# Ordering attention-value matmuls by key block over four PSUM slots, with a re-planned instruction list

## The chip, the cores and the metric

One core of one Trainium2 chip. The metric is device microseconds of one execution; the runs before took 289.94 us in the median (289.79 to 290.12). Every execution also leaves a span, from its first to its last profiled instruction, which is shorter than the time (by 1.8 us in the profiled run before). TensorE is the engine that multiplies matrices, ScalarE (ACT) takes the exponentials, VectorE (DVE) the masks and normalisations.

## The reference, cut to what matters

```python
scores = scale * np.matmul(q, k.transpose(0, 1, 3, 2))     # q, k, v: 4 x 8 x 768 x 64
scores = np.where(mask, scores, -1000000000.0)             # window, edge and random blocks of 32
attn = exp(scores - max) / sum                             # [cut: softmax]
x = np.matmul(attn, v)                                     # -> 3072 tokens x 512
gate = 1.0 / (1.0 + np.exp(-(x @ w_gate)))                 # 512 x 1536
return (gate * (x @ w_val)) @ w_out
```

Of the kernel before, what the change touches and what calls it, by code (L numbers as in the profile page):

```python
# [18 lines left out]
NJ = S // 128  # L19
# [8 lines left out]
VW = 96  # L28
SPIN = 22.0
NMASK = 1  # L30
SEED, MIX = 43, 0.4
WANT, READY = 4, 1
Q0P, M1P, M2P = -39.2, 14, 17
XR, HR, HOLD, HN = 3, 2, 0.4, 1
# [236 lines left out]
def kernel(  # L271
# [33 lines left out]
    P = Plan()  # L305
# [11 lines left out]
    def sb(tag, shape, dt):  # L317
        n = len(P.rings[tag])
        return Buf(tag, lambda i: work.tile(shape, dt, tag=tag, bufs=n, name=tag))
# [4 lines left out]
    def psb(shape, dt=f32, homes=SINGLE, span=1):  # L324
        def make(i):
            t = psum[:, i : i + span].rearrange("p b c -> p (b c)")
            if dt != f32:
                t = t.bitcast(dt)
            n = int(np.prod(shape))
            t = t[:, 0:n]  # L330
            if len(shape) == 2:
                t = t.rearrange("p (a b) -> p a b", a=shape[0])
            return t

        b = Buf("ps", make)
        b.homes, b.span = homes, span
        return b
# [23 lines left out]
    for i, (eng, q, r) in enumerate((("SP", nc.sync, 0), ("ACT", nc.scalar, 64))):  # L361
# [3 lines left out]
            writes=[e24], prio=-93, dma=0.2, lands=LAND[f"e{i}"],  # L365
        ).deps[1:] = []
    vring = [one([128, 2, NJ, VW], f16, f"v16_{i}") for i in range(8)]
    for i in range(8):
# [3 lines left out]
            writes=[vring[i]], prio=-80 + i,  # L372
# [15 lines left out]
    stage, half16, tr, v16 = {}, {}, {}, {}  # L388
    landed = {}

    def load(nm, b, p, prio, after=(), sync=None, behind=()):
        t = sb(f"{nm}s", [128, 2, NJ, 64], f32)
        stage[nm, b, p] = t

        def go():
            ins = nc.sync.dma_start(t(), src[nm][b][:, 2 * p : 2 * p + 2])
            if sync is not None:
                tc.add_manual_dep(
                    ins.ins, landed[sync].ins.name,
                    mybir.DependencyInfo(mybir.DependencyClass.Sync, mybir.DependencyReason.DATA),  # L400
                    reason="later loads",
                )

        return P.op("SP", 0.5, go, writes=[t], prio=prio, after=after, behind=behind, dma=1.07)
# [111 lines left out]
    n = 0  # L516
    for a, z in zip(edges, edges[1:]):
        for nm, t, s in (("g", wg, wgv), ("v", wv, wvv)):
# [4 lines left out]
            o = P.op("POOL", 0.75, go, prio=-37.5 + n * 0.75, behind=[last_in], dma=32 * (0.022 + (z - a) * 0.000124))  # L523
# [100 lines left out]
    valued, scored = {}, []  # L624

    def attend(n, p, seq):
        b, c = divmod(n, NCH)
        masked = n < NMASK
        pts = []
        for tt in range(NCH):  # L630
            st, pt = psb([2, 512], homes=PAIR, span=2), sb("pt", [128, 2, 2, CH], f16)

            def scores(tt=tt, st=st):
                qT, kT = tr["q", b, p](), tr["k", b, p]()
                for jj in range(2):
                    for own in (0, 1) if masked else (1,):
                        for hd in range(2):
                            r = slice(hd * 64, hd * 64 + 64)
                            l, m = (kT, qT) if own else (e24(), bias())
                            nc.tensor.matmul(  # L640
                                st()[:, hd, jj * CH : (jj + 1) * CH],
                                l[r, 2 * tt + jj, :],
                                m[r, 2 * c : 2 * c + 2, :],
                                start=not (own and masked), stop=bool(own),
                            )

            need = [tr["q", b, p], tr["k", b, p]]
            o = P.op(
                "PE", 0.43 if masked else 0.215, scores, reads=[*need, e24, bias] if masked else need,
                writes=[st], prio=seq, mode="row", behind=scored[-1:],  # L650
            )
            if (n, p, tt) == (0, 0, 0):
                o.deps.remove(late)
            scored.append(o)
            o.paired, o.twin = (n, p) not in EARLY and 4 * n + p < CHAIN, psb([2, 512], homes=PAIR, span=2)
            P.op(
                "ACT", 0.915,
                lambda st=st, pt=pt: nc.scalar.activation(  # L658
                    pt().rearrange("p h j q -> p h (j q)"), st(), AF.Exp, scale=SCALE
                ),  # L660
                reads=[st], writes=[pt], prio=seq,
            )

            def masks(tt=tt, pt=pt):
                t = pt().rearrange("p h j q -> p h (j q)")
                nc.vector.tensor_tensor(  # L666
                    t, t, mask()[:, c, tt].unsqueeze(1).to_broadcast([128, 2, 512]), op=ALU.mult
                )

            if not masked:  # L670
                P.op("DVE", 0.61, masks, reads=[pt], writes=[pt], after=[mask_ops[c, tt]], prio=seq)
            pts.append(pt)

        o, rz, x16 = psb([4, 128]), sb("rz", [128, 4, 1], f32), sb("x16", [128, 2, 128], f16)

        def values():
            v_ = v16[b, p]()
            for jq in range(2):
                for hd in range(2):
                    for j in range(NJ):  # L680
                        nc.tensor.matmul(  # L681
                            o()[:, 2 * jq + hd, 0:65],
                            pts[j // 2]()[:, hd, j % 2, jq * 128 : jq * 128 + 128],
                            v_[:, hd, j, 0:65],
                            start=(j == 0), stop=(j == NJ - 1),
                        )

        valued[n, p] = P.op("PE", 0.79, values, reads=[*pts, v16[b, p]], writes=[o], prio=seq + (3.05 if n == 0 and p < 3 else 0.1), mode="full")
        hold = HOLD if n < HN else 0.0
        P.op(  # L690
            "DVE", 0.2, lambda: nc.vector.reciprocal(rz(), o()[:, :, 64:65]), reads=[o], writes=[rz], prio=seq - 5  # L691
        ).hold = hold
        P.op(
            "DVE", 0.36,
            lambda: nc.vector.tensor_tensor(  # L695
                x16().rearrange("p j (h d) -> p (j h) d", d=64),
                o()[:, :, 0:64],
                rz().to_broadcast([128, 4, 64]),
                op=ALU.mult,
            ),  # L700
            reads=[o, rz], writes=[x16], prio=seq - 5,
        ).hold = hold
        g, i = group_of[n]
        dst = xT[g, p]
        if n >= TURN_PE:
            P.op(
                "SP", 1.2,
                lambda: nc.sync.dma_start_transpose(
                    dst()[:, i * CH : (i + 1) * CH].rearrange("p (j q) -> p j q", j=2),
                    x16().rearrange("p j m -> p (j m)"),  # L710
                ),
                reads=[x16], writes=[dst], prio=seq - 5, dma=0.45,
            )
            return
        tT = psb([2, 128], f16)

        def turn():
            dst()
            for jq in range(2):
                nc.tensor.transpose(tT()[:, jq, :], x16()[:, jq, :], ident16())  # L720

        P.op("PE", 0.12, turn, reads=[x16, ident16], writes=[tT, dst], prio=seq - 5, mode="full").hold = hold
        P.op(
            "DVE", 0.28,
            lambda: nc.vector.tensor_copy(
                dst()[:, i * CH : (i + 1) * CH], tT().rearrange("p j q -> p (j q)")
            ),
            reads=[tT], writes=[dst], prio=seq - 5,
        ).hold = hold
# [90 lines left out]
    seq, turned, late_loads = 0, [], []  # L820
    order = [(n, p) for n in range(B * NCH) for p in range(NP)]
    order = EARLY + [i for i in order if i not in EARLY]
    for n, p in order:
        b, c = divmod(n, NCH)
# [10 lines left out]
        if p == NP - 1 and b + 1 < B and c == 0:  # L835
            for p in range(NP):
                for nm in "kqv":
                    o = load(
                        nm, b + 1, p, seq + p, behind=turned[:-2][-2:],
                        **(dict(after=[w_out[4]], sync="o") if b == 0 else {}),  # L840
                    )
# [71 lines left out]
```

## The kernel before: what the change and the argument touch

The kernel records operations with planned durations. A planner then walks in time through these durations and fixes the order of instructions on each engine. Priorities get a random shift, drawn from a seed, so that the seed and the durations together choose the list. Where TensorE has nothing to do before 22 us, the planner inserts a filler matmul on zeros (44 in the trace of before, the last at 22.4 us).

One attention block is one chunk of 256 queries of one pair of heads. It has three score tiles (768 keys), whose exponentials lie in `pts`, and then one values block: 24 matmuls, each 128 keys by 128 queries times 65 columns. Column 65 of `v` is ones, so that it sums the denominators. The four results (two query tiles times two heads) lie in four slots of one PSUM bank.

```python
SEED, MIX = 43, 0.4
...
def run(self):
    mix = np.random.default_rng(SEED).normal(0.0, MIX, len(self.ops))
    for i, o in enumerate(self.ops):
        o.key = (o.prio + (mix[i] if -45 < o.prio < 60 else 0.0), i)
...
def spin_op(dur, fresh):                       # the filler, "L380"
    ...
    return P.op("PE", dur, lambda: nc.tensor.matmul(t()[0:64], zero()[:, 0:64], zero(), start=True, stop=True), ...)
...
o, rz, x16 = psb([4, 128]), ...                # four slots of 128 columns in one bank

def values():                                  # "L681"
    v_ = v16[b, p]()
    for jq in range(2):
        for hd in range(2):
            for j in range(NJ):                # NJ = 6 key blocks
                nc.tensor.matmul(
                    o()[:, 2 * jq + hd, 0:65],
                    pts[j // 2]()[:, hd, j % 2, jq * 128 : jq * 128 + 128],
                    v_[:, hd, j, 0:65],
                    start=(j == 0), stop=(j == NJ - 1),
                )

valued[n, p] = P.op("PE", 0.79, values, reads=[*pts, v16[b, p]], writes=[o], ...)
```

`start` is given to the matmul that begins a sum; I call that a clear, and here a block has four. L640 are the score matmuls, L746 the gate and value products of the feed-forward part, L791 its output product, L720 and L457 transposes.

The softmax here doesn't subtract the row's maximum and nothing guards it: scores larger than these inputs give would overflow.

## Time and profile before

| | |
|---|---|
| time, median of 3 | 289.94 us |
| span of the profiled run | 288.5 us |
| TensorE busy, matmuls | 98% of the span, 3030 |
| values matmuls (L681) | 1152, in 48 blocks of 24 |
| a values block, start to next start | 0.73 us |
| a steady period (one attention block and its share of the feed-forward part) | 5.48 us |
| fillers (L380) | 44 |

The prediction below shows the lines behind most of these. For a full engine the step from one start to the next start is the cost; a row's own duration overlaps what follows (the values row at 153.84 us is 0.89 us long, and the next row starts after 0.73 us).

These are the first score matmuls in the timeline of the kernel before (start in us, duration in us, engine, line, operation, output and inputs, count):

```profile
6.30 0.28 PE L640 MATMUL psum<-bias,e 64*128 64x256 f16 x2
6.42 0.27 PE L640 MATMUL psum<-qT,kT 64*128 64x256 f16 x2
6.53 0.27 PE L640 MATMUL psum<-bias,e 64*128 64x256 f16 x2
6.64 0.27 PE L640 MATMUL psum<-qT,kT 64*128 64x256 f16 x2
...
8.00 0.41 PE L457 MATMUL psum<-ident,q_late 128*64 128x128 f16 x8
```

Pairs of score matmuls, whose two members start 3 to 4 ns apart, follow each other every 0.11 us here, and the twelve pairs are over at 8.0 us.

### The profile page before, as it was taken

How to read it: one execution, taken by the hardware profiler on the slowest of the kernel's cores; microseconds unless marked ns; L12 is line 12 of the kernel's file. 1: busy time of each engine (PE TensorE's matmuls, PEld its weight loads, DVE VectorE, ACT ScalarE, POOL GpSimd, SP SyncE). 2: the span in 40 equal slices, each digit the busy share in tenths (PEclk: the TensorE clock that was granted, in tenths of full speed). 3: DMA queues.
4: the chain of work that ended last, by engine and by line, in shares of the span. 5: the costliest groups of instructions: out<-in, count | busy, mean ns of one | idle time of the engine just before them, and what ended most of it. 6: DMA issues, size and time to landing. Idle time of an engine off the chain costs nothing.

```text
span 288.5 us, 7279 instructions
## 1 busy us (share of the span) xinstructions
PE 282.4 (98%) x3030; PEld 172.7 (60%) x3030; DVE 186.7 (65%) x401; ACT 204.3 (71%) x281; POOL 14.9 (5%) x24
## 2 busy tenths in 40 slices
PE   7998999999999999999999999999999999999995
PEld 6686786787578555555555555554555555447753
DVE  3788997898897876876586575476476474223310
ACT  3969879987897898886888886876776773333321
POOL 8740000000000000000000000000000000000000
PEclk9999999999999999999999999999999999999999
DMA  7999999992799982061867661101011012001013
GB/s 111 171 207 211 208 242 257 239 286 57 220 211 172 258 203 50 18 184 36 227 179 161 218 69 56 33 25 55 21 38 55 11 47 57 36 36 36 19 56 111
DMA packets 50785, 35.25 MB, mean 122 GB/s; under 512 B 31376, under 2 KB 47808, under 8 KB 50752
## 3 DMA queue, kind: packets, MB, share of 16 engines
q1 hardware_dynamic: 43304, 27.71, 37.5%
q0 software_dynamic: 7232, 7.01, 15.2%
q8 instruction: 23, 0.38, 0.6%
q10 hardware_dynamic: 216, 0.07, 0.1%
q14 instruction: 10, 0.08, 0.1%
HBM read 28.42 MB, written 6.29 MB: 120 GB/s over the span
## 4 chain that ended last, share of the span: by engine, by line
PE 93%; DMA 2%; ACT 2%; POOL 2%; issue 0%; ACTq 0%; POOLq 0%
PE psum L746 44%; PE psum L791 23%; PE psum L640 13%; PE psum L681 12%; DMA q<-in_q_dram 2%; ACT pt L658 1%; PE psum L457 1%; PE psum L720 1%; POOL k L439 0%; PE psum L602 0%; POOL k_a L486 0%; POOL q_late L439 0%; POOL q L439 0%; POOL k_b L490 0%; PE psum L380 0%
## 5 line engine op out<-in xcount | busy, mean ns | idle before, releaser
L658 ACT ACTIVATE pt<-psum 128x1024 f16<-128x1024 f32 x144 | 138.8, 1029 | 25.1 <-PE psum L640 25.1
L666 DVE TENSOR_TENSOR pt<-pt,mask 128x1024 f16<-128x1024 f16 x132 | 88.9, 686 | 45.7 <-ACT pt L658 45.6
L746 PE MATMUL psum<-x,wv 128*128 128x256 f16 (+1 forms) x384 | 78.2, 326 | 0.0
L746 PE MATMUL psum<-x,wg 128*128 128x256 f16 (+1 forms) x384 | 78.2, 326 | 0.0
L767 ACT ACTIVATE tg<-psum 128x256 f32<-128x256 f32 (+1 forms) x96 | 47.6, 499 | 41.7 <-PE psum L746 30.6
L791 PE MATMUL psum<-wo,h 128*128 128x512 f16 (+2 forms) x300 | 73.0, 371 | 0.0
L774 DVE SCALAR_TENSOR_TENSOR h<-tg,psum 128x256 f16<-128x256 f32 (+1 forms) x96 | 52.2, 550 | 28.8 <-PE psum L746 16.1
L746 PEld LDWEIGHTS <-wg 128*128 128x128 f16 x384 | 35.9, 98 | 24.3 <-issue 1.7
L746 PEld LDWEIGHTS <-wv 128*128 128x128 f16 x384 | 35.3, 98 | 23.0 <-issue 2.5
L681 PEld LDWEIGHTS <-pt 128*128 128x128 f16 x1152 | 41.0, 97 | 8.8 <-issue 1.1
L640 PE MATMUL psum<-qT,kT 64*128 64x256 f16 x576 | 45.0, 271 | 0.5 <-ACT pt L658 0.4
L791 PEld LDWEIGHTS <-h 128*128 128x128 f16 x300 | 26.3, 98 | 30.2 <-issue 5.7
L681 PE MATMUL psum<-v,pt 128*128 128x65 f16 x1152 | 42.7, 193 | 0.3 <-ACT pt L658 0.3
L640 PEld LDWEIGHTS <-kT 64*128 64x128 f16 x576 | 24.5, 94 | 18.6 <-issue 15.4
L695 DVE TENSOR_TENSOR x<-psum,rz 128x256 f16<-128x256 f32 x48 | 20.4, 424 | 1.7
L809 ACT ACTIVATE y<-psum 128x512 f32<-128x512 f32 (+2 forms) x22 | 12.7, 579 | 10.9 <-PE psum L791 10.8
L691 DVE RECIPROCAL rz<-psum 128x4 f32<-128x4 f32 x48 | 8.6, 179 | 4.9 <-PE psum L681 4.8
L380 PE MATMUL psum<-zero 128*64 128x128 f16 x44 | 6.1, 287 | 1.0 <-DVE zero L350 1.0
L427 ACT CAST q<-qs 128x768 f16<-128x768 f32 x8 | 6.8, 845 | 0.0
L610 DVE TENSOR_SCALAR mask<-psum 128x512 f16<-128x512 f32 x9 | 6.0, 684 | 0.5 <-PE psum L640 0.5
L640 PE MATMUL psum<-bias,e 64*128 64x256 f16 x48 | 6.0, 273 | 0.0
L380 PEld LDWEIGHTS <-zero 128*64 128x64 f16 x44 | 4.6, 155 | 2.1 <-issue 1.1
(54 smaller groups left out, 72.3 us busy)
## 6 DMA issues: line engine op xcount, KB each, us to landing
out_dram<-y SPq DMA_DIRECT2D x23, 256.0 KB, 2.0
qs<-in_q_dram SPq DMA_DIRECT2D x12, 384.0 KB, 3.8
vs<-in_v_dram SPq DMA_DIRECT2D x12, 384.0 KB, 4.9
ks<-in_k_dram SPq DMA_DIRECT2D x12, 384.0 KB, 4.5
wg<-in_moe_w_gate_dram POOLq DMA_DIRECT2D x2, 768.0 KB, 13.9
wv<-in_moe_w_val_dram POOLq DMA_DIRECT2D x2, 768.0 KB, 16.0
wo<-in_moe_w_out_dram POOLq DMA_DIRECT2D x3, 512.0 KB, 21.9
vh<-in_v_dram POOLq DMA_DIRECT2D x4, 192.0 KB, 8.1
```

What stands on the lines that cost most here:

```text
L380: "PE", dur, lambda: nc.tensor.matmul(t()[0:64], zero()[:, 0:64], zero(), start=True, stop=True),
L640: nc.tensor.matmul(st()[:, hd, jj * CH : (jj + 1) * CH], l[r, 2 * tt + jj, :], m[r, 2 * c : 2 * c + 2, :], start=not (own and masked), sto ...
L658: lambda st=st, pt=pt: nc.scalar.activation(pt().rearrange("p h j q -> p h (j q)"), st(), AF.Exp, scale=SCALE),
L666: nc.vector.tensor_tensor(t, t, mask()[:, c, tt].unsqueeze(1).to_broadcast([128, 2, 512]), op=ALU.mult)
L681: nc.tensor.matmul(o()[:, 2 * jq + hd, 0:65], pts[j // 2]()[:, hd, j % 2, jq * 128 : jq * 128 + 128], v_[:, hd, j, 0:65], start=(j == 0), ...
L691: "DVE", 0.2, lambda: nc.vector.reciprocal(rz(), o()[:, :, 64:65]), reads=[o], writes=[rz], prio=seq - 5
L695: lambda: nc.vector.tensor_tensor(x16().rearrange("p j (h d) -> p (j h) d", d=64), o()[:, :, 0:64], rz().to_broadcast([128, 4, 64]), op=AL ...
L746: nc.tensor.matmul(t()[:, z : z + w], wt()[:, i, f * 128 : (f + 1) * 128], xT[g, i]()[:, 0:w], start=(i == 0), stop=(i == NP - 1),)
L767: lambda tg=tg, a=pair[0]: nc.scalar.activation(tg()[:, 0:w], a[0]()[:, a[1] : a[1] + w], AF.Tanh, scale=0.5),
L774: lambda tg=tg, a=pair[1], h_=h_: nc.vector.scalar_tensor_tensor(h_()[:, 0:w], tg()[:, 0:w], 1.0, a[0]()[:, a[1] : a[1] + w], op0=ALU.add, ...
L791: nc.tensor.matmul(py()[:, m], hts[g, f]()[:, tt * 128 : (tt + 1) * 128], wo()[:, f, m], start=(f == 0), stop=(f == NF - 1),)
L809: lambda py=py, y=y, m=m: nc.scalar.activation(y()[:, m], py()[:, m], AF.Copy, scale=0.5),
```

## The change

Its intent: six matmuls in a row that add to the same 65 columns were thought to be slower than matmuls that go round over the four slots. All four sums are now open at once in one bank, and the first matmul alone has `start`. The planned duration of a block goes down with it, and with a new seed the planner makes another list.

```diff
-SEED, MIX = 43, 0.4
+SEED, MIX = 3, 0.4
...
-            for jq in range(2):
-                for hd in range(2):
-                    for j in range(NJ):
+            for j in range(NJ):
+                for jq in range(2):
+                    for hd in range(2):
                         nc.tensor.matmul(
                             o()[:, 2 * jq + hd, 0:65],
                             pts[j // 2]()[:, hd, j % 2, jq * 128 : jq * 128 + 128],
                             v_[:, hd, j, 0:65],
-                            start=(j == 0), stop=(j == NJ - 1),
+                            start=(j + jq + hd == 0), stop=(j == NJ - 1), skip_group_check=True,
                         )
...
-        valued[n, p] = P.op("PE", 0.79, values, ...
+        valued[n, p] = P.op("PE", 0.715, values, ...
```

More of the change, by code (lines that the diff above doesn't have):

```diff
@@ L684, in values @@
                             v_[:, hd, j, 0:65],
-                            start=(j == 0), stop=(j == NJ - 1),
+                            start=(j + jq + hd == 0), stop=(j == NJ - 1), skip_group_check=True,
                         )
-        valued[n, p] = P.op("PE", 0.79, values, reads=[*pts, v16[b, p]], writes=[o], prio=seq + (3.05 if n == 0 and p < 3 else 0.1), mode="full")
+        valued[n, p] = P.op("PE", 0.715, values, reads=[*pts, v16[b, p]], writes=[o], prio=seq + (3.05 if n == 0 and p < 3 else 0.1), mode="full")
         hold = HOLD if n < HN else 0.0
```

## The prediction

> **What bounds the kernel now.** I read the page's busy shares first, then the slices, the chain that ended last, the waits of TensorE, and last the timeline of one period of the steady part. The first two lines and the slices of the page:
>
> ```profile
> span 288.5 us, 7279 instructions
> ## 1 busy us (share of the span) xinstructions
> PE 282.4 (98%) x3030; PEld 172.7 (60%) x3030; DVE 186.7 (65%) x401; ACT 204.3 (71%) x281; POOL 14.9 (5%) x24
> ...
> PE   7998999999999999999999999999999999999995
> ...
> PEclk9999999999999999999999999999999999999999
> ```
>
> TensorE (PE) is busy 98% of the span at a full granted clock, and only the first slice (loads still under way) and the last (copying out the end) fall short. The chain says the same:
>
> ```profile
> PE 93%; DMA 2%; ACT 2%; POOL 2%; issue 0%; ACTq 0%; POOLq 0%
> PE psum L746 44%; PE psum L791 23%; PE psum L640 13%; PE psum L681 12%; DMA q<-in_q_dram 2%; ACT pt L658 1%; PE psum L457 1%; PE psum L720 1%; POOL k L439 0%; PE psum L602 0%; POOL k_a L486 0%; POOL q_late L439 0%; POOL q L439 0%; POOL k_b L490 0%; PE psum L380 0%
> ```
>
> 93% of the chain is matmuls; the changed ones, the values matmuls of L681, are 12%, that is 0.12 x 288.5 = 35 us for 48 blocks of 24, or 0.72 us a block. All waits of TensorE together are five:
>
> ```profile
> PE psum L380 <- DVE zero L350: 1.0, 1, 1.0
> PE psum L578 <- DMA e<-bb_e: 0.6, 1, 0.6
> PE psum L640 <- ACT pt L658: 0.4, 1, 0.4
> PE psum L457 <- DMA k<-in_k_dram: 0.4, 1, 0.4
> PE psum L681 <- ACT pt L658: 0.3, 1, 0.3
> ```
>
> That is 2.7 us of idle, 2.0 of it in the first 10 us where loads rule. The two waits on ACT are at 24.8 and 27.4 us; in the table of busy time by stages TensorE has no idle time at all between 30 and 240 us. So a better list order can win back at most about 0.7 us of idle, and the rest of any gain must come from matmuls that take less time. One steady period:
>
> ```profile
> 153.40 0.60 PE L791 MATMUL psum<-wo,h 128*128 128x512 f16 x2
> 153.84 0.89 PE L681 MATMUL psum<-v,pt 128*128 128x65 f16 x24
> 154.57 1.02 PE L746 MATMUL psum<-x,wv 128*128 128x512 f16 x4
> 155.44 1.03 PE L746 MATMUL psum<-x,wg 128*128 128x512 f16 x4
> ...
> 159.32 0.89 PE L681 MATMUL psum<-v,pt 128*128 128x65 f16 x24
> ```
>
> The block's line (L681, 153.84) is to be read by its start: its 0.89 us includes its drain, which overlaps the next block; what the block costs the stream is the step to the next start, 154.57 - 153.84 = 0.73 us. The whole period is 159.32 - 153.84 = 5.48 us.
>
> [...] starts of L746 with 256 columns lie 109 ns apart [...], with 512 columns 216 ns [...]. [...] the trace's values blocks take 729 to 730 ns in the steady part, so 730/24 = 30.4 ns[...]. [...] each weight load of L681 starts about 2 ns after the matmul before it starts, and no matmul waits for one by record. [...]
>
> **Part 1: the order inside a values block.** Nothing is removed: 24 weight loads of 128x128 and 24 matmuls of 65 columns before and after, 1152 in all, with the same operands. Before, six matmuls in a row add to the same 65 columns; after, the same columns come round every fourth matmul [...]. Three first clears a block go, but in the trace's start-to-start steps those matmuls (7th, 13th, 19th) take no longer than others: a clear costs nothing visible. What is visible is a pattern: steps of 29 ns, and one of 35 after every four or so, while the records' durations creep from 191 to 196 ns between the long steps and fall back after each. I read this as issue at 29.2 ns a matmul into something downstream that takes 30.4 ns each, which pushes back now and then. Two candidates: the add to an address written one matmul ago (then the new order removes it), or the pace of weight loads and small outputs as such (then nothing changes).
> If it is the add, the block falls[...]; if issue alone is left, to 24 x 29.2 = 700 ns, 29 ns less. The planned figure in the diff (0.79 to 0.715) is not a measured step: before measures 0.73, not 0.79, so the 0.075 of the diff can't be what comes out[...].
> On the path: five blocks of L681 lie before 28 us, where ACT's exponentials set the pace (the chain gives 4.3 us to them from 23.45 us), so 43 of 48 count. [...] at most 43 x 0.029 = 1.25.
>
> **Part 2: the list order.** The built programs have equal counts of every matmul but the filler one: 44 before, 47 after. The fillers (L380) run where the planner finds nothing else, before 23 us; 3 more, at some 0.1 us, sit in time that is waited anyway, and one more pair of array-mode changes comes with them. Changes between full-array and row-paired matmuls cost about 95 ns each in the trace (a 512-column matmul takes 312 ns to the next start in place of 216). There are 55 + 53 = 108 of these in either program, so the new order saves none. From the fully chained part on (after about 125 us) the block order is the same in both. Between 20 and 125 us blocks are permuted. This can shift the 0.3 and 0.4 us waits on ACT, or make new ones: ACT is busy 22 of 25 us at 100 to 125 us, and DVE 18 of 20 at 60 to 80 us, so there is not much room. I put the sum at 0 with a spread of some 0.6 us, leaning to a small win since the plan now carries shorter times for TensorE's work.
> The tail, from the last matmul to the end, is unchanged: 288.5 - 285.3 = 3.2 us.
>
> Sum: [...] some 0.25 us for the list: 0.8 us off 289.94, so **289.1 us**.
>
> **Rivals.** First, order doesn't matter to the array: 30.4 ns is what a weight load and a small matmul take together. For it: the long steps come about every fifth matmul and do not line up with the slot borders at every sixth, where the same-address add is absent; weight-load records creep (96 to 100 ns) along with the matmuls. Against it: none shows as a wait. Time then 289.9, give or take the list. Second, the diff's own numbers are right and a block loses 0.075 us: 48 x 0.075 = 3.6 us, so 286.3 us. Against it: 0.73 - 0.075 = 0.655 us is 27.3 ns a matmul[...]. Third, the permuted middle part opens waits on ACT or DVE, of up to a few tenths each: 290 to 291 us. For it: ACT's and DVE's busy shares above; against it: the old plan, made with the same planner, left TensorE no idle there, and values that are really shorter only make the engine less hurried than planned. Fourth, key-block order lets the first eight matmuls start with the first score tile alone; but the wait before L681 is 0.3 us in the whole run, so this is worth nothing.
>
> **Range and chances.** Low end: all long steps gone (1.25) and the waits on ACT won back (0.7) is 288.0; 287.9 with a little over. High end: no gain, and 0.5 us of new waits: 290.4. Faster by over 2% would need 284.1 us, 5.8 us less, more than even the second rival; slower by over 2% needs 5.8 us of new waits in a part that has none. One chance in a hundred each.
>
> **What will show it.** The step from a values block to the next block (0.73 us in the steady part) should read 0.71, and the steady period 5.46 in place of 5.48; if both are unchanged, the first rival holds; at 0.66 and 5.41 the second. The long steps of 35 ns should be fewer or gone. TensorE's waits on ACT should stay at or below 0.7 us in sum; new rows after 30 us mean the third rival. Bank clears, mode changes, the tail and the first 12 us should be as before. The prediction is wrong if same-address adds cost nothing and the list brings waits, or if something else in the middle part gains more than the 0.7 us of idle that I see there.

The sum came to 0.8 us off 289.94: 0.56 for the loop order and some 0.25 for the list. The 0.56 was my estimate, two chances in three of a shorter block in 43 of the 48; the pace for a matmul of 65 columns that it rested on was not shown. The 0.71 and 5.46 us under "What will show it" rest on it too. The trace of before allows an estimate of its own: matmuls of 128 columns (L791) follow each other every 56 ns, of 256 (L746) every 109, of 512 every 216, so about 0.42 ns a column, and 63 columns fewer than 128 leave 56 - 26.5 = 29.5 ns, or 708 for a block; measured are 30.4 and 729 or 730. Against the second rival, which needs 27.3 ns a matmul, stands that no step inside a steady block of that trace is under 29 ns. That something downstream pushes back was a reading of the step times, which no run showed.

## The result, and the profile after

The changed kernel took 291.89 us in the median of four runs (291.54 to 292.31), against 290.02 us (289.79 to 290.12) for four runs of the kernel before. The ratio was 1.0066, with a 95% interval of 1.0049 to 1.0084. That is within 2%, slower instead of faster, and outside the predicted range.

The first check is the block itself. One steady period of the changed kernel, from its timeline:

```profile
149.50 0.90 PE L681 MATMUL psum<-v,pt 128*128 128x65 f16 x24
150.23 1.02 PE L746 MATMUL psum<-x,wg 128*128 128x512 f16 x4
...
154.99 0.90 PE L681 MATMUL psum<-v,pt 128*128 128x65 f16 x24
```

The period is now 154.99 - 149.50 = 5.49 us; before it was 5.48. From the trace's start times in ns, a steady block takes 735, where before it took 729 or 730. The block has not become shorter by 20 ns but longer by 6. The pauses of 35 ns are still there, and there is one more of them (steps between the 24 starts, and to the next block, of one block each):

```
before 30 35 29 29 29 29 35 29 30 29 29 35 29 29 29 30 35 29 29 29 29 35 29 | 30
after  29 35 29 29 29 35 29 30 29 35 29 29 29 29 35 30 29 29 29 35 29 29 30 | 35
```

The second check is TensorE's waits in the changed kernel (who waited for whom; us in total, times, longest):

```profile
PE psum L380 <- DVE zero L350: 1.0, 1, 1.0
PE psum L720 <- DVE x L695: 0.7, 1, 0.7
PE psum L578 <- DMA e<-bb_e: 0.6, 1, 0.6
PE psum L457 <- DMA k_b<-in_k_dram: 0.3, 1, 0.3
PE psum L681 <- ACT pt L658: 0.3, 1, 0.3
```

Their sum is 2.8 us by the trace's ns (the rows are rounded); it was 2.7. One wait for ACT (0.4 us before L640) has become one for DVE before a transpose (0.7 us before L720, at 27.7 us). After 30 us there is again no wait: the permuted middle part opened none.

The third check is where the span grew by 1.0 us. I cut both profiled runs at matmuls that both have: the first values matmul, the first feed-forward matmul (L746), the first matmul of the 48th values block, and the last matmul of all.

| us | before | after |
|---|---|---|
| span's start to first values matmul | 14.47 | 15.57 |
| to the first L746 | 13.66 | 13.79 |
| to the 48th values block | 212.54 | 212.54 |
| to the last matmul | 44.42 | 44.43 |
| last matmul to the span's end | 3.46 | 3.19 |
| time beyond the span | 1.8 | 2.8 |

From the first values matmul to the last matmul the two differ by 0.15 us (270.61 and 270.76). The whole loss lies before and after that: 1.1 us at the start and 1.0 us beyond the span's end. The start looks like this in the changed kernel's timeline:

```profile
6.15 0.64 PE L457 MATMUL psum<-ident,k_b 128*64 128x128 f16 x8 [0.28 <-DMA k_b<-in_k_dram]
6.58 0.42 PE L380 MATMUL psum<-zero 128*64 128x128 f16 x2
6.93 0.39 PE L640 MATMUL psum<-bias,e 64*128 64x256 f16 x2
7.12 0.42 PE L640 MATMUL psum<-qT,kT 64*128 64x256 f16 x2
7.34 0.42 PE L640 MATMUL psum<-bias,e 64*128 64x256 f16 x2
7.55 0.42 PE L640 MATMUL psum<-qT,kT 64*128 64x256 f16 x2
...
9.96 0.41 PE L457 MATMUL psum<-ident,q_late 128*64 128x128 f16 x8
```

The same instructions in the same order, since the lists part only later, now follow each other every 0.21 us, at half the rate, and the scores are over at 9.96 us in place of 8.00. The trace has its first record of the full clock at 10.0 us; in the profile of before it is at 5.6 us. (The page's clock row shows full speed in this slice too: it has no record before that one, so it can't be trusted there. The steps are what tells it.) The profiles thus show half the rate, and a moment that varies: the first record of the full clock is at 5.6 us in `before` and at 10.0 here, and at 9.6 and 9.4 us in two profiles further down (`pairs` and `list_minus3`). What brings the full clock was not shown. Its record lasts 283.31 us in `before` and 279.89 here.

So there were three suspects: the loop order, the list, and things at the two ends of a run that may or may not belong to the change.

### The profile page after: what moved, and what is told of

It is laid out like the page before. It is cut to its first block, busy times and chain, and to the rows that moved or that the text cites. A ratio compares the mean times of both kernels' runs of the same rounds, so it can differ in the third digit from the quotient of the medians.

```text
span 289.5 us, 7286 instructions
## 1 busy us (share of the span) xinstructions
PE 283.7 (98%) x3033; PEld 173.4 (60%) x3033; DVE 186.9 (65%) x402; ACT 204.7 (71%) x280; POOL 14.8 (5%) x24
## 4 chain that ended last, share of the span: by engine, by line
PE 96%; DMA 1%; ACT 1%; issue 0%; POOL 0%; DVE 0%; ACTq 0%; DVEq 0%; POOLq 0%
PE psum L746 44%; PE psum L791 22%; PE psum L640 14%; PE psum L681 12%; DMA k_b<-in_k_dram 1%; PE psum L457 1%; PE psum L720 1%; PE psum L380 1%; ACT pt L658 1%; PE psum L602 0%; POOL k_a L486 0%; DVE x L695 0%; ACT y L809 0%; PE psum L578 0%; DVE rz L691 0%
## 5 line engine op out<-in xcount | busy, mean ns | idle before, releaser
L746 PE MATMUL psum<-x,wg 128*128 128x256 f16 (+1 forms) x384 | 78.2, 326 | 0.0
L746 PE MATMUL psum<-x,wv 128*128 128x256 f16 (+1 forms) x384 | 78.1, 326 | 0.0
L791 PE MATMUL psum<-wo,h 128*128 128x512 f16 (+2 forms) x300 | 72.9, 371 | 0.0
L746 PEld LDWEIGHTS <-wg 128*128 128x128 f16 x384 | 35.7, 98 | 23.8 <-issue 2.1
L746 PEld LDWEIGHTS <-wv 128*128 128x128 f16 x384 | 35.7, 98 | 22.7 <-issue 1.7
L640 PE MATMUL psum<-qT,kT 64*128 64x256 f16 x576 | 45.5, 274 | 0.0
L791 PEld LDWEIGHTS <-h 128*128 128x128 f16 x300 | 26.4, 98 | 30.4 <-issue 5.7
L640 PEld LDWEIGHTS <-kT 64*128 64x128 f16 x576 | 24.7, 95 | 18.5 <-issue 15.7
L809 ACT ACTIVATE y<-psum 128x512 f32<-128x512 f32 (+2 forms) x20 | 11.5, 577 | 11.0 <-PE psum L791 10.8
L380 PE MATMUL psum<-zero 128*64 128x128 f16 x47 | 6.7, 289 | 1.0 <-DVE zero L350 1.0
L640 PE MATMUL psum<-bias,e 64*128 64x256 f16 x48 | 7.0, 307 | 0.0
```

The lines of the kernel that those rows point to most:

```text
L640: nc.tensor.matmul(st()[:, hd, jj * CH : (jj + 1) * CH], l[r, 2 * tt + jj, :], m[r, 2 * c : 2 * c + 2, :], start=not (own and masked), sto ...
L746: nc.tensor.matmul(t()[:, z : z + w], wt()[:, i, f * 128 : (f + 1) * 128], xT[g, i]()[:, 0:w], start=(i == 0), stop=(i == NP - 1),)
L791: nc.tensor.matmul(py()[:, m], hts[g, f]()[:, tt * 128 : (tt + 1) * 128], wo()[:, f, m], start=(f == 0), stop=(f == NF - 1),)
L809: lambda py=py, y=y, m=m: nc.scalar.activation(y()[:, m], py()[:, m], AF.Copy, scale=0.5),
```

## The experiments

### Loop order and list apart, and the same kernel again

`list_only` is the changed kernel with the old loop. The built program equals the changed one on every engine, but for the order of the 24 matmuls in a block and for the clears.

```diff
-SEED, MIX = 43, 0.4
+SEED, MIX = 3, 0.4
-        valued[n, p] = P.op("PE", 0.79, values, ...
+        valued[n, p] = P.op("PE", 0.715, values, ...
```

> The values loop of the kernel before, with the re-planned list (program equal to the changed kernel but for the order of 24 matmuls in a block and three clears). Theory A (the list, or what comes with its program, carries the loss): about 291.6 us, steps of a values block back at 730 ns. Theory B (the loop order carries it): about 290.0 us. By the traces the loop order costs 6 ns in each of 48 blocks, 0.3 us, so A is expected for most of the 1.9 us.

`loop_only` is the reverse: the new loop and the single clear, with seed 43 and the planned 0.79, so that the list is exactly that of before.

```diff
-            for jq in range(2):
-                for hd in range(2):
-                    for j in range(NJ):
+            for j in range(NJ):
+                for jq in range(2):
+                    for hd in range(2):
-                            start=(j == 0), stop=(j == NJ - 1),
+                            start=(j + jq + hd == 0), stop=(j == NJ - 1), skip_group_check=True,
```

> The list of the kernel before, exactly, with the new loop order and one clear a block. Theory A (list): 290.0 + 43 blocks x 6 ns = 290.3 us, values block 735 ns, steady period 5.487 us. Theory B (loop order): about 291.5 us. The first 12 us: if the half-rate matmuls between 7 and 10 us come with the list they are absent here; if they are chance of the run they may be here too.

`after_again` is the changed kernel, unaltered (no edit).

> The changed kernel unaltered, for the spread of its start. Theory C (the slow start at 7 to 10 us, half-rate matmuls after a late key load, is a chance of the profiled run): some profile of these has matmuls at full rate there, a span near 288.6 us. Theory D (it belongs to this program): the slow start is here again, time 291.5 to 292.3 us.

`one_clear` is the kernel before with its own order, and `start` only on the first matmul of a block.

```diff
-                            start=(j == 0), stop=(j == NJ - 1),
+                            start=(j + jq + hd == 0), stop=(j == NJ - 1), skip_group_check=True,
```

> The kernel before with its loop order and list kept, and start given only on the first matmul of a block. If clears cost nothing, as the steps of the trace say: 290.0 us, block 730 ns. If each clear had cost some 6 ns: 48 x 18 ns = 0.9 us less.

All four gave right results. They shared one chip and eleven runs of the kernel before (median 290.76 us, 290.05 to 291.37):

| kernel | median of 6, us | ratio to before | 95% interval | block, ns |
|---|---|---|---|---|
| list_only | 290.75 | 1.0003 | 0.9979 to 1.0027 | 729 |
| loop_only | 290.80 | 1.0006 | 0.9988 to 1.0025 | 735 |
| after_again | 291.42 | 1.0017 | 0.9994 to 1.0039 | 735 |
| one_clear | 290.84 | 1.0004 | 0.9986 to 1.0022 | 729 or 730 |

Neither theory A nor theory B of the loss holds: no part alone carries 1.9 us, and the whole change itself came out at a quarter of the first ratio. The kernel before now varied by 1.3 us between runs, where its first three had lain within 0.33. In the profile of `after_again` the scores ran at full rate:

```profile
6.36 0.28 PE L640 MATMUL psum<-bias,e 64*128 64x256 f16 x2
6.48 0.27 PE L640 MATMUL psum<-qT,kT 64*128 64x256 f16 x2
...
8.05 0.41 PE L457 MATMUL psum<-ident,q_late 128*64 128x128 f16 x8
8.30 0.38 PE L578 MATMUL psum<-e,mb 128*64 128x512 f16 x2
8.52 0.22 PE L380 MATMUL psum<-zero 128*64 128x128 f16 x1
9.59 0.53 PE L457 MATMUL psum<-ident,k 128*64 128x128 f16 x12 [0.86 <-DMA k<-in_k_dram]
```

Theory C, chance, is the right one for the half-rate start. What chance took from this run was less: a key load landed late (a wait of 0.86 us where the profile of before has 0.37), and the first values matmul began at 15.00 us.

What does belong to the change shows where chance has no part. The way from the first L746 to the 48th values block, with 42 values blocks between, took 212.54 us in the kernel before, 212.37 in `list_only`, 212.75 in `loop_only` and 212.54 in `after_again`. The new loop order costs 0.17 us (after_again against list_only) or 0.21 us (loop_only against before), and 42 blocks by 5 to 6 ns are 0.21 to 0.25. With the new list this is firm: its profiles, those further down too, gave 212.53 to 212.54 us with the new loop (four of them) and 212.36 to 212.37 with the old one (three). With the old list it is not: kernels with that list and blocks of 729 or 730 ns (some of them below) lay between 212.38 and 212.73 us. So the 0.17 us that the new list seems to give back there is not shown either. Clears cost nothing that shows: 729 or 730 ns with one as with four.

One thing remained from the first result: the time beyond the span. In the eleven runs of before it was 1.74 to 2.03 us. In `list_only` and `after_again` it was 2.67 to 2.88 in two runs of six each, and it had been 2.25 to 2.94 in all four of the first runs. The trace's record of transfers has something to match. In the three profiles at hand of this list (2.7 to 2.8 us beyond the span) an instruction packet of 16 KB comes after the span's end, which no profile of the old list shows:

```
               span   last instruction packets, us from the span's start (KB)
before         288.5  266.12 (16)   282.36 (8)   285.72 (8)
loop_only      288.4  265.99 (16)   282.33 (8)   285.64 (8)
after          289.5  265.97 (16)   286.29 (8)   290.48 (8)   291.40 (16)
```

The page's transfer rows do not show it; they count to the span's end:

```profile
q8 instruction: 23, 0.38, 0.5%
```

The 23 packets of 16 KB on this queue are 0.38 MB, in before as in after. Which engine's instructions they bring is not in the trace. TensorE has by far the longest list (6078 instructions in the trace of before; DVE, the next, has 488), so I take the queue to be TensorE's, which is a guess. The changed kernel has three more fillers, so six more matmuls and weight loads (6085 instructions in its trace). How many instructions a packet holds was not shown, so there is no reason known why six of them should matter; the next runs try it.

### Six TensorE instructions more, or fewer

`before_plus3` adds three fillers in TensorE's idle time before the first L578 (a matmul on the mask); `after_minus3` leaves out three of the changed kernel's, those at 21.4 us.

```diff
+    fills = []
+
+    def fill(t):
+        fills.append(t)
+        for _ in range(2 if len(fills) <= 3 else 1):        # before_plus3
+            nc.tensor.matmul(t()[0:64], zero()[:, 0:64], zero(), start=True, stop=True)
...
+        if len(fills) in (43, 44, 45):                      # after_minus3, in place of the loop
+            return
```

> The kernel before with three more filler matmuls (6 more TensorE instructions, the count of the changed kernel) in TensorE's idle 0.6 us before the first expand; nothing else. In all profiles of the re-planned list two instruction packets, one of 16 KB, come 1 to 2 us after the span's end, and the time exceeds the span by 2.7 to 2.8 us in place of 1.8. Theory E (the six extra TensorE instructions push the end of the program over a fetch boundary): such packets here too, and some runs with time minus span near 2.8. Theory F (it is another engine's count or chance): no such packets, time minus span 1.8 in all runs, median as before.

> The changed kernel without three of its filler matmuls (those at 21.4 us, where TensorE waits), so with the TensorE instruction count of before. Theory E: no instruction packets after the span's end, time minus span 1.8 in all runs, median 0.3 to 0.9 us under the changed kernel's. Theory F: packets after the end still there, some runs at 2.7 or more.

`before_plus3` took 290.97 us (median of 6; ratio 1.0021, interval 0.9990 to 1.0051), and two of its six runs had 2.58 and 2.64 us beyond the span. The fillers themselves cost nothing in that place (270.57 us from the first values matmul to the last matmul). Its profiled run has the 16 KB packet, at 287.54 us, here inside the span; that run's span was 290.9 because SyncE waited until 289.8 us for the last output write, which I have not explained. `after_minus3` took 290.43 us (ratio 0.9998, 0.9973 to 1.0023), its six runs lay between 1.82 and 1.89 beyond the span, and its profile has no late 16 KB packet (an 8 KB one comes at 289.43, after the end, without harm). Of theories E and F, E is the one that these two runs support.

It is not the whole truth, as later runs show. Over all runs, 10 of 28 with the longer TensorE list had 2.25 us or more beyond the span, and 3 of 83 with the shorter one (2.32, 2.67 and 2.88). Four of the ten are the first comparison; without it there are 6 of 24. So a long end was more frequent with the longer list, but the count is neither necessary nor sufficient for it, and why it comes in one run and not in the next stays open. That the packet itself delays the end was not shown by taking it away alone; its coming after the end and the 0.9 us go together in the four profiles of this list and length (three have both, and one, further down, has neither).

The fillers left out also won something on the chain. From the first values matmul to the first L746 `after_minus3` took 13.63 us where the changed kernel took 13.79 (with the old loop, 13.60 and 13.62 against 13.78). The planner had put them where it saw idle time, but TensorE was not idle there long enough.

### What the 30 ns of a values matmul are

`pairs` goes round over two slots in place of four. `width49` and `width64` narrow the matmuls from the second key block on to 49 and 64 columns (wrong results); `width66` widens all to 66, with a second column of ones (right result).

```diff
# pairs
             for jq in range(2):
-                for hd in range(2):
-                    for j in range(NJ):
+                for j in range(NJ):
+                    for hd in range(2):
-                            start=(j == 0), stop=(j == NJ - 1),
+                            start=(j + jq + hd == 0), stop=(j == NJ - 1), skip_group_check=True,
# width49 (width64: 64 in place of 49; v_ is cut alike)
-                            o()[:, 2 * jq + hd, 0:65],
+                            o()[:, 2 * jq + hd, 0 : 65 if j == 0 else 49],
# width66 (v_ is cut alike)
-            lambda i=i: nc.vector.memset(vring[i]()[:, :, :, 64:65], 1.0),
+            lambda i=i: nc.vector.memset(vring[i]()[:, :, :, 64:66], 1.0),
-                            o()[:, 2 * jq + hd, 0:65],
+                            o()[:, 2 * jq + hd, 0:66],
```

> The list of before; key blocks ordered over two slots at a time, so that the slot changes with every matmul but the same address comes round every second one. Theory G (a change of slot at each matmul costs the 6 ns a block, whatever the distance): 735 ns a block as in the changed kernel. Theory H (it depends on the distance or on the weight addresses): 729, or another value than either.

> The kernel before with only 49 of 65 columns from the second key block on (wrong result on purpose; 20 of 24 matmuls a block are 16 columns, 6.7 ns, shorter). Theory I (the step is set by the columns): 24 x 30.4 - 20 x 6.7 = 596 ns a block. Theory J (weight loads or another fixed pace set it): the block stays near 700 to 730 ns.

> The kernel before with 64 columns from the second key block on (wrong denominators on purpose). If columns count: 730 - 20 x 0.42 = 722 ns a block, pauses as before. If the pauses belong to widths that are not a multiple of some unit: near 690 ns, no pauses.

> The kernel before with 66 columns in every values matmul (one more column of ones; the result stays right). If the 6 ns pauses come from the odd number of columns: [...]. If columns simply count, 0.42 ns each: 740 ns and 290.6 us.

A steady block took 729 ns in `pairs`, 625 in `width49`, 710 in `width64` and 729 in `width66`. The times of the first three are single runs (291.35, 285.59 and 289.98 us); `width66` took 290.67 us (ratio 0.9999, 0.9974 to 1.0024). The timelines of width66 and of width49 around a block:

```profile
148.80 0.89 PE L681 MATMUL psum<-v,pt 128*128 128x66 f16 x24
149.53 1.03 PE L746 MATMUL psum<-x,wg 128*128 128x512 f16 x4
```

```profile
150.97 0.78 PE L681 MATMUL psum<-v,pt 128*128 128x65 f16 x24
151.59 1.02 PE L746 MATMUL psum<-x,wv 128*128 128x512 f16 x4
```

The block of width66 is 0.73 us long, that of width49 0.62 (its row names the first form, 65 columns). None of the three widths gave a block length that had been expected for it. What follows:

- Adding again to the address just written costs nothing that shows. In `pairs` no matmul does so any more, and the block is as long as before (729 ns). Changing the slot at each matmul costs nothing by itself either; only the round over four slots has the one pause more (735 ns). Whether slots, weights' or `v`'s addresses make it was not told apart, so theory H is right only in that distance or addresses matter.
- A column more (66) costs nothing, and a column less (64) takes (729 - 710) / 20 = 0.95 ns off each of the 20 narrowed matmuls. Two columns take 0.84 ns in this kernel's wide matmuls (216 ns for 512 columns, 109 for 256, so 0.42 ns each). That is as if widths counted by twos, with 65 paid as 66; only 64, 65 and 66 were tried, and the cause was not shown. With 66 columns a matmul takes 729 / 24 = 30.4 ns as well. So the pauses do not come from the odd width: an even one has them as well.
- Between 65 and 49 columns the block does not fall by the 20 x 6.7 = 134 ns of theory I but by 104, and no step of a steady block is under 25 ns. So near 65 columns the width still counts (64 are 0.95 ns shorter); at 49 the steps stay at 25 ns or more, and what holds them there was not shown.
- What makes the pauses of 35 ns stays open: they are there at 64, 65 and 66 columns, in all three orders, and with one clear or four. In `width49` they are gone: most of its steady blocks have steps of 29 ns for the four matmuls of 65 columns, one step of 31, and 25 or 26 for all others.

The profile of `pairs`, with the list of before, also had the slow start: its first record of the full clock is at 9.6 us, its first values matmul at 15.35.

```profile
6.77 0.40 PE L640 MATMUL psum<-bias,e 64*128 64x256 f16 x2
6.96 0.42 PE L640 MATMUL psum<-qT,kT 64*128 64x256 f16 x2
7.17 0.42 PE L640 MATMUL psum<-bias,e 64*128 64x256 f16 x2
```

So such a start does not need the new list. Three of the fifteen profiles have it: `after` and `list_minus3` (below) with the new list, `pairs` with the old. That is too few to say whether one list has it more often.

### The list without the other two, and the change once more

`list_minus3` is the new list with the old loop and the three fillers of 21.4 us left out: what is left of the change when both costs are taken away.

```diff
-SEED, MIX = 43, 0.4
+SEED, MIX = 3, 0.4
+        if len(fills) in (43, 44, 45):        # in fill(t), as in after_minus3
+            return
-        valued[n, p] = P.op("PE", 0.79, values, ...
+        valued[n, p] = P.op("PE", 0.715, values, ...
```

> The re-planned list with the old loop order and three fillers fewer (TensorE count of before). If the loss of the changed kernel is the sum of loop order (6 ns a block), late instruction packets and a start that varies by chance, then this is as fast as the kernel before within 0.2 us: first values matmul to last matmul 270.6 us as before, time minus span 1.8 us in all runs.

> The re-planned list, old loop order, three fillers fewer, once more, since it looked 0.2% faster than the kernel before. If that is its shorter way from first values matmul to last matmul (270.4 to 270.6 us against 270.6): ratio 0.999 to 1.000. If the list is really worth 0.5 us or more: ratio 0.998 or less again.

> The changed kernel once more. If its lasting loss is the loop order (0.26 us) and late instruction packets in a part of the runs (0.9 us in 4 or so of 10), with a start that is slow by chance in either kernel: ratio 1.001 to 1.003, spans of both kernels in the same two groups (288.2 to 288.9 and 289.2 to 289.6). If the first comparison's 1.0066 is the kernel's own: ratio 1.005 or more, spans of 289.3 and over in most runs of it alone.

`list_minus3` took 290.14 us (ratio 0.9980, 0.9960 to 1.0000), and run again as `list_minus3_b` 290.59 us (ratio 1.0004, 0.9988 to 1.0020). Inside, both profiles agree: 270.39 and 270.40 us from the first values matmul to the last matmul, against 270.61 before. That would be 0.2 us, 0.1%, but the kernel before was profiled once, other kernels with its list and a like block lay between 270.45 and 270.81, and the timed runs can't confirm it. No version that I have is clearly faster than before. The expectation that every run would be 1.8 us beyond the span failed: one had 2.88. The profile of the first one had the half-rate start too (full clock from 9.4 us, first values matmul at 15.27).

`after_third`, the changed kernel for the third time, took 290.92 us (ratio 1.0018, 1.0002 to 1.0034), close to `after_again`. None of its six runs exceeded 2.12 us beyond the span, and its profile, at 1.84 us, has no 16 KB packet after the end, though it is the same program. Its cut times are those of the first profile: 13.79, 212.53 and 44.43 us. Only the ends differ, with a first values matmul at 14.55 us.

The spans tell what chance did. In these repeats 15 of 44 runs of the kernel before and 6 of 12 of the changed kernel had spans of 289.2 us or more, the rest 288.0 to 289.1. In the first comparison it was three of four for the changed kernel, and none of four for the kernel before (its times less 1.8 us are 288.0 to 288.3). So of the first 1.9 us, about 1.0 came from spans, most of it a start that either kernel may have, and about 0.9 from the time beyond the span, which was long in four runs of four then and in 2 of 12 later. What is left in the repeats is 1.0017 and 1.0018, 0.5 us, though the first interval (from 0.9994) includes no loss at all, and the second (from 1.0002) only just excludes it. Inside, from the first values matmul to the last matmul, the changed kernel is 0.14 to 0.15 us longer in all three of its profiles. The rest lies at the two ends, and how much of that belongs to the change is not shown.

## Why the prediction was wrong, point by point

**The bound** was right. TensorE sets the time, no wait appeared after 30 us, and the middle part is the same within 0.2 us.

**Part 1 failed in its choice.** I gave two chances in three to "the add to an address written one matmul ago". The pauses have nothing to do with it: `pairs` removes every such add and stays at 729 ns, and the changed order itself goes to 735. The block of 0.71 us was the wrong target as well: 65 columns take the time of 66 (729 ns a block in both). The term of the sum was thus a loss of about 0.2 us (6 ns a block; 0.17 us over 42 blocks with the new list) where I had put a gain of 0.56 on average. The observation that the long steps do not line up with the slot borders, which I noted for the first rival, was the evidence, and I let the planned 0.715 outweigh it. Rival one, that nothing changes, was nearly right; it had no place for six ns more. Rival two fell at once. What I said of the clears held (729 or 730 ns a block with one as with four).

**Part 2 was right that the list alone changes little, and wrong on a gain from it and on the fillers.** The new list alone is even with the old one (ratio 1.0003, and 270.57 against 270.61 us from the first values matmul to the last matmul), where I had put a gain of 0.25 us. But I wrote that three more fillers "sit in time that is waited anyway". They cost 0.16 us before the first L746 (13.79 against 13.63 us), and with the count that they bring a long end was more frequent, for a reason that stays open.

**Rival three** did not occur: one of the two waits at 25 to 28 us changed its cause, with 0.95 us for both in place of 0.72, and no new one came.

**The range failed for a reason of its own.** Its upper end, 290.4 us, was built from changes in the middle of the run alone, with nothing for the spread between runs (the three runs known then lay within 0.33 us). I had written that the first 12 us and the tail would be as before. Neither the start, whose half rate and late loads move the first values matmul by about 1 us with either list (14.47 us in `before` and 15.35 in `pairs`, 14.55 in `after_third` and 15.57 in the first profile of the changed kernel), nor the time beyond the span, was a term of the sum. The upper end would have been exceeded by 28 of 44 repeats of the unchanged kernel too.

## What to carry to other kernels

Before reordering small matmuls against a supposed cost of repeated adds, look at whether the slow steps line up with those adds; here they did not, and taking the adds away showed that they were free (729 ns a block with and without them). Three runs within 0.1% are not the spread of a kernel whose start differs from run to run (a pair of score matmuls every 0.11 or every 0.21 us, a wait of 0.37 or 0.86 us for a key load): cut the traces at common instructions, compare the parts, and repeat before explaining an end. When a plan adds instructions to fill idle time, check on the trace that the time was idle (here three fillers cost 0.16 us), and look at the end of the run too, since the program has become longer.
